# Input combinations and first weights queued singly behind the dense layer, the third block's denominators one dense block earlier, and the last rows inside the first pair

## The chip, the core and the metric

The kernel runs on one core of a Trainium2 chip. The metric is the device time of one execution in microseconds (us). Three runs of the kernel before gave 2571.55, 2571.56 and 2573.55 us; their median is 2571.56 us.

The engines are named as in the profile: PE does matmuls (PEld is its weight load), DVE is the vector engine, ACT the scalar engine, POOL the one called GpSimd, and SP issues most of the DMAs. Each engine takes its instructions in a fixed order, so an instruction that waits keeps back everything behind it on that engine.

## What is computed

Two kinds of layer alternate over 2048 rows of 576 features: linear attention with a softmax feature map, and a dense layer with a squared ReLU. Both are applied twice, with the same weights.

```python
def _A_ref(x, wqkv, w_phi, wo):                    # 32 heads of 18
    q, k, v = split(x @ wqkv)
    pq, pk = q @ w_phi, k @ w_phi                  # per head
    phi_q = concat([softmax(pq), softmax(-pq)])
    phi_k = concat([softmax(pk), softmax(-pk)])
    kv, z = phi_k.T @ v, sum_over_rows(phi_k)      # per head
    den = phi_q @ z + 1e-6
    return ((phi_q @ kv) / den) @ wo

def _B_ref(x, w1, b1, w2, b2):                     # 576 -> 4608 -> 576
    r = relu(x @ w1 + b1)
    return (r * r) @ w2 + b2

x = x + _A_ref(layernorm(x), ...)
x = x + _B_ref(layernorm(x), ...)
x = x + _A_ref(layernorm(x), ...)
x = x + _B_ref(layernorm(x), ...)
```

## The kernel before

**Blocks and order.** The 2048 rows are four blocks of 512 (`TB`), each of four tiles of 128 rows. In layer 0 the dense layer runs over the blocks in the order 3, 2, 0, 1. Layer 1 takes them in the order 1, 0, 3, 2: blocks 1 and 0 go through `g_mlp` one after the other, blocks 3 and 2 together through `g_pair`. In the profile's names `m_1` and `m_0` are the dense blocks of row blocks 1 and 0 (of either layer, as buffer numbers are left out), `a_3` and `a_2` the attention of blocks 3 and 2, and `m_p` the pair. Here "the first dense block" and "the second dense block" mean block 1 and block 0 in layer 1.

**Split numbers.** To keep fp32 accuracy, each matmul operand is split into a rounded high part and the rest, and three products are added. So each operand costs ACT a copy (the high part) and DVE or POOL a subtraction (the rest).

**`g_mlp` (L684).** 36 chunks `f` of 128 hidden features. `first(f)` loads and splits one chunk's weights (DMAs at L695 to L697, ACT L702 and L703, DVE L705 and L706, POOL L707). `hidden(f)` makes 14 products into PSUM bank `h` (L717). `square(f)` empties that bank with a ReLU on ACT (L724), squares it twice on ACT (L725, L726) and takes the rest on DVE (L727); the last of these is kept as `dense["last"]`. `second(f - 1)` adds to five PSUM banks, `acc0` to `acc4` (L735, L744). After each chunk it yields. At the end the features' bank is turned (`m_0py`, L780), added to the rows loaded into `x` tiles (L783, L784), the last chunk's row products for tiles 0 and 1 and then for tiles 2 and 3 follow (L776, L786), and four rows are stored (L789).

**`weave` (L99).** The dense block is the main generator and everything else is traced between its yields. Each yield adds `rate` to a credit, and steps of the other generator are taken while the credit is at least 1; a step costs what it yields (`paced` sets that).

```python
due += rate
while due >= 1.0:
    cost = next(other, other)
    if cost is other:
        break
    due -= cost or 1.0
```

In layer 1 the rates are 3.0 for the first dense block and 4.8 for the second. Costs: 5.5 for one tile's softmax (`g_soft`), 2.8 for each of the eight half-steps of the denominators (`g_phi`: sums over the features, reciprocals, and scaling), 1.0 for a step of queries or of the attention's output (`g_out`), and 3.0 for a step of the norm behind it. A dense block has 36 turns (two after chunk 0, then one a chunk).

**Order.** A scheduler places the traced instructions on each engine by when it holds them ready, the earlier traced ones first. `tc.issue_after(ins)` adds an edge of order alone: what the block traces on `ins`'s engine stands behind `ins` in that engine's queue. `held` (L560) wraps every step of a generator in one such edge, behind `dense["last"]`, so on DVE alone.

**What rides on the second dense block.** For block 3: denominators, output, and `g_norm_first`. For block 2: queries, softmax, denominators, output, and `g_norm_second`. The latter has ten steps: four tiles of rows with their norm, then main steps 0 and 1, a tail, main steps 2 and 3, a tail. A main or tail step turns normed rows on PE into one of the two `w` banks (L814, L822) and makes input combinations of blocks 3 and 2 from them (`combine`: DVE L895 to L900, POOL L901 and L903), each of which is split (L886, L887, L913, L914). Last, `next(pair)` (L1266) runs the first part of `g_pair`: pair 0's weights are loaded (`load_pair`, L937 and L939, ten DMAs) and all seven operands made and split in one go (`split_pair`; POOL sums L970, L972, L975, L977; ACT L962, DVE L963, POOL L965 for each split), and pair 1's weights are loaded.

**`g_pair` (L925).** 18 pairs of chunks. With the combined inputs, seven products (`product`, L997) give a pair's hidden features of both blocks. Three banks are used: `bx` in `h`, `by` and `bz` in the two `w` banks. `bx` is read by DVE between products (L1091, L1100, L1104) that go on adding to it. The next pair's `split_pair` is a generator `prep` with one yield: four splits after the product `s1`, three after `a22`. Its sums are `x` tiles, of which there are five in all; the dense block's end takes four of them.

Of the kernel before, what the change touches and what calls it, by code (L numbers as in the profile page):

```python
# [21 lines left out]
def layers_kernel(  # L22
# [661 lines left out]
    def g_mlp(layer, b, x, after, name, behind=None):  # L684
# [34 lines left out]
        def square(f):  # L719
# [6 lines left out]
            nc.scalar.activation(hr, hr, AF.Square)  # L726
# [54 lines left out]
        for t in range(NT):  # L781
# [3 lines left out]
            after.append(x)  # L785
        by_rows(NF - 1, range(2, NT), range(3))  # L786
# [138 lines left out]
    def g_pair(layer, blocks, x, after, name):  # L925
# [17 lines left out]
        def split_pair(k, raw):  # L943
# [28 lines left out]
            nc.gpsimd.tensor_sub(ss[1], ss[0], a11)  # L972
            split("s2", ss[1])
            yield
            nc.gpsimd.tensor_sub(ss[3], a12, ss[1])  # L975
            split("s4", ss[3])
            nc.gpsimd.tensor_sub(ss[2], a11, a21)  # L977
            split("s3", ss[2])
            split("a22", a22)

# [99 lines left out]
        for k in range(NP):  # L1080
            f0, f1 = 2 * k, 2 * k + 1
            prep = split_pair(k + 1, raw) if k + 1 < NP else iter(())
            bx = ps_a.tile([P, TB], F32, tag="h", name=f"{name}px{k}")
            by = ps_w.tile([P, TB], F32, tag="w", name=f"{name}py{k}")
            bz = ps_w.tile([P, TB], F32, tag="w", name=f"{name}pz{k}")
            load_wide(f0)
            product(k, bx, "a11", "b11", True)
            product(k, by, "a12", "b21", True)
            z = sb.tile([P, TB], F32, tag="hr", name=f"{name}z{f0}", bufs=2)
            nc.scalar.activation(z, by, AF.Copy)  # L1090
            nc.vector.scalar_tensor_tensor(z, bx, bias(f0), z, op0=ALU.add, op1=ALU.add)  # L1091
            nc.scalar.activation(z, z, AF.Relu)
            square(f0, z)
            product(k, bz, "s1", "t1", True)
            next(prep, None)
            product(k, bx, "s2", "t2", False)
            u = sb.tile([P, D], F32, tag="qk", name=f"{name}u{f0}", bufs=5)[:, :TB]
            v = sb.tile([P, D], F32, tag="qk", name=f"{name}u{f1}", bufs=5)[:, :TB]
            nc.scalar.activation(v, bz, AF.Copy)
            nc.vector.tensor_add(u, bx, v)  # L1100
            product(k, by, "s4", "b22", True)
            product(k, bx, "s3", "t3", False)
            nc.vector.scalar_tensor_tensor(u, by, bias(f0), u, op0=ALU.add, op1=ALU.add)
            nc.vector.scalar_tensor_tensor(v, bx, bias(f1), v, op0=ALU.add, op1=ALU.add)  # L1104
            nc.scalar.activation(u, u, AF.Relu)
            nc.scalar.activation(u, u, AF.Square)
            nc.sync.dma_start(hd[f0], u)
            keep_high(f1, v)
            if k:
                second(f0 - 1)  # L1110
            load_wide(f1)
            product(k, bx, "a22", "t4", False)
# [4 lines left out]
            if k + 2 < NP:  # L1117
                raw = load_pair(k + 2)
# [4 lines left out]
        for f in range(NF, NF + 2):  # L1123
            load_wide(f)
            load_high(f)
# [184 lines left out]
```

## Time and profile before

| | value |
|---|---|
| median of 3 runs | 2571.56 us |
| the profiled execution | 2570.49 us |
| its span on the core | 2568.8 us |
| mean granted clock of PE | 0.993 |
| busy in the span: PE, PEld | 2508.2 us (98%), 2205.1 us (86%) |
| DVE, ACT, POOL | 1536.7 us (60%), 1266.5 us (49%), 801.5 us (31%) |
| DMA | 295.03 MB, mean 115 GB/s |

In this trace the first dense block runs from about 1528 to 1798 us, the second from 1798 to 2126 us, the 18 pairs of features from 2126 to 2452 us, and block 2's rows from there to the end.

How to read the lines. In a table of stretches each row has the stretch, its length, the busy time of PE, PEld, DVE, ACT and POOL with their instructions, the granted clock, the DMA share and GB/s. A row of waits has the engine and line that waited, whom for, and total, times and longest in us. A row in order of time has start, duration, engine, line, operation, output and inputs, and in brackets the idle time before it and what ended it. A row of the chain of waits has start, duration and what. PE's ends are modelled and matmuls overlap, so the distance between starts tells more than a duration.

### The profile page before, as it was taken

The numbers are of one execution on the slowest core, as the hardware profiler recorded it, in microseconds if no ns is written. First come the engines' busy times: TensorE is split into PE (matmuls) and PEld (weight loads), VectorE is DVE, ScalarE is ACT, GpSimd is POOL, SyncE is SP. The second block draws the span as 40 slices with busy tenths as digits, with TensorE's granted clock in tenths as the row PEclk, the third lists the DMA queues.
The fourth block names the chain that finished last, engine by engine and source line by source line (L and its number), as shares of the span: only waits on it lengthen the run. The fifth ranks groups of instructions, "written<-read, shape, count | busy, mean of one in ns | idle before, by whom it ended". The sixth has DMA issues, their size and how long they took to land.

```text
span 2568.8 us, 41380 instructions
## 1 busy us (share of the span) xinstructions
PE 2508.2 (98%) x15282; PEld 2205.1 (86%) x15282; DVE 1536.7 (60%) x2408; ACT 1266.5 (49%) x2177; POOL 801.5 (31%) x869
## 2 busy tenths in 40 slices
PE   8998999999999999999999999999999989999999
PEld 8998888888888888888888988888888877888888
DVE  7778844456665467556434787464757765555444
ACT  4344554445554455545544445454545456666543
POOL 3444311113222133223111433112223256555222
PEclk9999999999999999999999999999999999999999
DMA  8103333354333543343333143333453434333364
GB/s 251 57 23 92 102 111 91 109 185 129 92 92 113 171 126 98 88 138 99 111 100 100 45 146 105 89 89 107 141 176 90 124 93 132 115 99 104 103 204 152
DMA packets 276758, 295.03 MB, mean 115 GB/s; under 512 B 28906, under 2 KB 206826, under 8 KB 274250
## 3 DMA queue, kind: packets, MB, share of 16 engines
q1 hardware_dynamic: 275296, 289.68, 37.6%
q8 instruction: 119, 1.95, 0.3%
q10 hardware_dynamic: 1258, 2.70, 0.3%
q14 instruction: 85, 0.70, 0.1%
HBM read 249.39 MB, written 42.89 MB: 114 GB/s over the span
## 4 chain that ended last, share of the span: by engine, by line
PE 52%; DVE 6%; POOL 1%; issue 1%; ACT 1%; DMA 0%; DVEq 0%; ACTq 0%; POOLq 0%; SPq 0%
PE m_1ph L717 9%; PE m_1acc L744 7%; PE m_0ph L717 5%; PE m_ppx L997 5%; PE m_pacc L1026 3%; PE m_0acc L744 3%; PE m_pacacc L1026 3%; PE m_ppy L997 2%; PE m_1acc L735 2%; PE m_ppz L997 1%; PE m_pacacc L1016 1%; PE m_pacc L1016 1%; PE m_0acc L735 1%; PE m_pach L1026 1%; PE a_0po L671 1%
## 5 line engine op out<-in xcount | busy, mean ns | idle before, releaser
L717 PE MATMUL m_0ph<-a_0nh,m_0h 128*128 128x512 f32 (+1 forms) x760 | 198.7, 389 | 8.2 <-ACT m_0hr L724 6.6
L744 PE MATMUL m_0acc<-m_0s,m_0hb 128*128 128x448 f32 x864 | 200.4, 367 | 3.7 <-DVE m_0hb L727 3.7
L744 PE MATMUL m_1acc<-m_1s,m_1hb 128*128 128x448 f32 x864 | 199.2, 366 | 0.5 <-DVE m_1hb L727 0.5
L744 PEld LDWEIGHTS m_0acc<-m_0s,m_0hb 128*128 128x128 f32 x864 | 161.3, 188 | 26.9 <-DVE m_0hb L727 6.0
L744 PEld LDWEIGHTS m_1acc<-m_1s,m_1hb 128*128 128x128 f32 x864 | 162.0, 188 | 21.4 <-DVE m_1hb L727 0.9
L717 PEld LDWEIGHTS m_0ph<-a_0nh,m_0h 128*128 128x128 f32 x760 | 137.5, 191 | 35.3 <-ACT m_0hr L724 7.5
L707 POOL TENSOR_TENSOR m_1s<-m_1r,m_1s 128x128 fp32r<-128x128 f32 x72 | 57.7, 801 | 334.8 <-ACT m_1s L703 298.1
L707 POOL TENSOR_TENSOR m_0s<-m_0r,m_0s 128x128 fp32r<-128x128 f32 x72 | 60.4, 838 | 312.9 <-ACT m_0s L703 280.6
L705 DVE TENSOR_TENSOR m_1h<-m_1r,m_1h 128x640 fp32r<-128x640 f32 x72 | 63.7, 885 | 145.8 <-ACT m_1h L702 145.8
L724 ACT ACTIVATE m_0hr<-m_0ph,b1t 128x512 f32<-128x512 f32 x72 | 49.3, 685 | 166.3 <-PE m_0ph L717 166.3
L705 DVE TENSOR_TENSOR m_0h<-m_0r,m_0h 128x640 fp32r<-128x640 f32 x72 | 65.7, 913 | 100.7 <-ACT m_0h L702 98.6
L724 ACT ACTIVATE m_1hr<-m_1ph,b1t 128x512 f32<-128x512 f32 x72 | 49.4, 685 | 148.5 <-PE m_1ph L717 148.5
L986 DVE TENSOR_TENSOR m_ps<-m_pr,m_ps 128x448 fp32r<-128x448 f32 x72 | 51.2, 711 | 95.8 <-ACT m_ps L985 94.9
L987 POOL TENSOR_TENSOR m_ps<-m_pr,m_ps 128x128 fp32r<-128x128 f32 x72 | 59.0, 819 | 136.2 <-ACT m_ps L985 128.1
L744 PE MATMUL m_2acc<-m_2s,m_2hb 128*128 128x448 f32 x432 | 99.7, 366 | 1.3 <-DVE m_2hb L727 1.3
L744 PE MATMUL m_3acc<-m_3s,m_3hb 128*128 128x448 f32 x432 | 99.6, 366 | 1.0 <-DVE m_3hb L727 1.0
L717 PE MATMUL m_1ph<-t1onh,m_1h 128*128 128x512 f32 (+1 forms) x380 | 97.1, 382 | 0.6 <-ACT t1onh L347 0.6
L717 PE MATMUL m_2ph<-a_2nh,m_2h 128*128 128x512 f32 (+1 forms) x380 | 97.2, 384 | 0.2 <-DVE m_2h L705 0.2
L717 PE MATMUL m_3ph<-t0onh,m_3h 128*128 128x512 f32 (+1 forms) x380 | 95.7, 382 | 0.1
L717 PE MATMUL m_1ph<-a_1nh,m_1h 128*128 128x512 f32 (+1 forms) x380 | 95.2, 381 | 0.0
L1026 PE MATMUL m_pacc<-m_ps,m_phb 128*128 128x448 f32 x432 | 94.1, 366 | 0.0
L985 ACT ACTIVATE m_ps<-m_pr 128x576 fp32r<-128x576 f32 x72 | 49.1, 683 | 88.6 <-PE m_pacacc L1016 63.7
(2103 smaller groups left out, 7121.2 us busy)
## 6 DMA issues: line engine op xcount, KB each, us to landing
m_0r<-in_B_w SPq DMA_DIRECT2D x72, 288.0 KB
m_1r<-in_B_w SPq DMA_DIRECT2D x72, 288.0 KB
m_pr<-in_B_w SPq DMA_DIRECT2D x72, 288.0 KB
m_0r<-in_B_w SPq DMA_DIRECT2D x72, 256.0 KB
m_1r<-in_B_w SPq DMA_DIRECT2D x72, 256.0 KB
m_3r<-in_B_w SPq DMA_DIRECT2D x36, 288.0 KB
m_2r<-in_B_w SPq DMA_DIRECT2D x36, 288.0 KB
m_3r<-in_B_w SPq DMA_DIRECT2D x36, 256.0 KB
```

Source lines behind the costliest of these rows:

```text
L705: nc.vector.tensor_sub(l1, r1, h1.bitcast(F32))
L707: nc.gpsimd.tensor_sub(s2[:, D + R : 2 * D], r2[:, R:], s2[:, R:D].bitcast(F32))
L717: nc.tensor.matmul(ph[:, cols], a, m, start=(k == 0), stop=(k == len(ops) - 1))
L724: nc.scalar.activation(hr, ph, AF.Relu, bias=b1t[:, f : f + 1])
L735: nc.tensor.matmul(acc[KC], a, m, start=(f == 0 and k == 0), stop=(f == NF - 1 and k == 2))
L744: nc.tensor.matmul(acc[t][:, :R], a[:, rows], m, start=(f == 0 and k == 0), stop=(f == NF - 1 and k == 2))
L985: nc.scalar.activation(s2[:, :D], r2, AF.Copy)
L986: nc.vector.tensor_sub(s2[:, D : D + R], r2[:, :R], s2[:, :R].bitcast(F32))
L987: nc.gpsimd.tensor_sub(s2[:, D + R : 2 * D], r2[:, R:], s2[:, R:D].bitcast(F32))
L997: nc.tensor.matmul(ps, a, m, start=start and i == 0, stop=i == len(ms) - 1, skip_group_check=True)
L1016: nc.tensor.matmul(accs[b][KC], a, m, start=(g == 0 and k == 0), stop=(g == NF - 1 and k == 2))
L1026: nc.tensor.matmul(accs[b][t][:, :R], a[:, rows], m, start=(g == 0 and k == 0), stop=(g == NF - 1 and k == 2))
```

## The change

1. `square` also keeps ACT's second square (L726) as `dense["squared"]`, and `held` takes a list of keys: its steps then stand behind the newest chunk's last subtraction on DVE and behind its second square on ACT.
2. `g_norm_second` is run through `held` with both keys.
3. `split_pair` yields after each of its seven splits, and POOL's sums are traced ahead of the split before the one that needs them. Pair 0's splitting is a generator of its own, `prelude`, run through `held` with both keys at a cost of 2.0 a step. In each pair the steps of `prep` are taken two after the first square, two after product `s1`, two before product `a22`, and the rest after it.
4. Block 3's denominators (`g_phi`, eight half-steps of 2.8) move from the second dense block to the first, behind block 3's softmax, which was there already.
5. The rates go from 3.0 to 3.6 for the first dense block and from 4.8 to 4.3 for the second.
6. At the end of the second dense block, ahead of the last chunk's row products for tiles 2 and 3, a new call `then` drains what is left of the side work and traces pair 0 up to its product `a22`. Pair 0 takes its five accumulators only after that.

```diff
-    def held(gen):
+    def held(gen, keys=("last",)):

         while True:
-            with tc.issue_after(dense["last"].ins):
+            with ExitStack() as behind:
+                for key in keys:
+                    behind.enter_context(tc.issue_after(dense[key].ins))
                 cost = next(gen, gen)
...
-            nc.scalar.activation(hr, hr, AF.Square)
+            dense["squared"] = nc.scalar.activation(hr, hr, AF.Square)
             dense["last"] = nc.vector.tensor_sub(hl, hr, hh.bitcast(F32))
...
             after.append(x)
+        if then:
+            then()
         by_rows(NF - 1, range(2, NT), range(3))
...
+            nc.gpsimd.tensor_add(ss[0], a21, a22)
             split("a11", a11)
+            yield
+            nc.gpsimd.tensor_sub(ss[1], ss[0], a11)
             split("a12", a12)
-            nc.gpsimd.tensor_add(ss[0], a21, a22)
+            yield
             split("s1", ss[0])
-            nc.gpsimd.tensor_sub(ss[1], ss[0], a11)
+            nc.gpsimd.tensor_sub(ss[3], a12, ss[1])
+            yield
             split("s2", ss[1])
-            yield
-            nc.gpsimd.tensor_sub(ss[3], a12, ss[1])
+            nc.gpsimd.tensor_sub(ss[2], a11, a21)
+            yield
             split("s4", ss[3])
-            nc.gpsimd.tensor_sub(ss[2], a11, a21)
+            yield
             split("s3", ss[2])
+            yield
             split("a22", a22)
+            yield
...
-        drain(split_pair(0, load_pair(0)))
-        raw = load_pair(1)
-        yield
-        accs[0] = [ps_a.tile([P, TB], F32, tag=f"acc{c}", name=f"{name}acc{c}") for c in range(NC)]
+        def prelude():
+            yield from split_pair(0, load_pair(0))
+            raws[1] = load_pair(1)
...
+                square(f0, z)
+                advance(prep, 2)
+                product(k, bz, "s1", "t1", True)
+                advance(prep, 2)
+                product(k, bx, "s2", "t2", False)
...
+                load_wide(f1)
+                advance(prep, 2)
+                if k == 0:
+                    yield
+                product(k, bx, "a22", "t4", False)
+                drain(prep)
...
+                if k == 0:
+                    accs[0] = [ps_a.tile([P, TB], F32, tag=f"acc{c}", name=f"{name}acc{c}") for c in range(NC)]
+                second(f0)
+                yield
...
+    def g_features(layer, raws, ph, name):
+        cost = (lambda c: c) if layer else (lambda c: None)
+        er = []
+        yield from paced(held(g_soft(raws, er, name)), cost(5.5))
+        yield from paced(held(g_phi(layer, er, ph, name, True)), cost(2.8))
...
-                    mid = (g_queries(layer, order[2], None, later, m), paced(held(g_soft(later, early, m)), 5.5))
+                    mid = (g_queries(layer, order[2], None, later, m), g_features(layer, later, early, m))
...
-                    yield from g_attend(layer, order[3], None, None, operands, f"a{layer}_{order[3]}", None, g_norm_second)
-                    next(pair)
+                    yield from g_attend(layer, order[3], None, None, operands, f"a{layer}_{order[3]}", None,
+                                        lambda *a: held(g_norm_second(*a), ("last", "squared")))
+                    yield from paced(held(prelude, ("last", "squared")), 2.0)
...
-            weave(g_mlp(layer, b, ready, rows, f"m{n}", None if i else dense["turned"]), g_back(), (3.0, 4.8)[i] if layer else 1.5 if i else 1.0)
+            back = g_back()
+
+            def then(back=back):
+                drain(back)
+                next(products)
+
+            weave(g_mlp(layer, b, ready, rows, f"m{n}", None if i else dense["turned"], then if layer and i == 1 else None),
+                  back, (3.6, 4.3)[i] if layer else 1.5 if i else 1.0)
```

More of the change, by code (lines that the diff above doesn't have):

```diff
@@ L681, in g_out, with g_mlp @@
         yield from paced((norm or g_norm)(x_after, dst, f"{name}n", keep), costs[1])
-    def g_mlp(layer, b, x, after, name, behind=None):
+    def g_mlp(layer, b, x, after, name, behind=None, then=None):
         xh, xl = x["h"], x["l"]
@@ L1134, in load_x @@
+        return prelude(), products()
     def load_x(b):
@@ L1148, in g_attend @@
                 yield from g_queries(layer, b, x, raws, name)
-            yield from paced(held(g_soft(raws, er, name)), cost(5.5))
-        ph = []
-        yield from paced(held(g_phi(layer, er, ph, name, True)), cost(2.8))
+            yield from g_features(layer, raws, ph, name)
         if mid[0]:
@@ L1231, in layers_kernel @@
         operands = {}
-        pair = g_pair(layer, order[2:], operands, None, f"m{layer}_p")
+        prelude, products = g_pair(layer, order[2:], operands, None, f"m{layer}_p")
         for i, b in enumerate(order):
```

110 lines of the change are left out of this document (53 added, 57 removed).

## The prediction

> **What bounds the kernel now.** I read the page first, then a table of stretches, then the matrix engine's waits, then the order of time around each wait. The page's first line gives the span; this execution took 2570.49 us in all (1.69 us lie around its span), 1.07 under the median 2571.56 of the three runs.
>
> ```profile
> span 2568.8 us, 41380 instructions
> ```
>
> In the table of stretches (us, then busy time per engine) layer 1's first dense block keeps PE busy throughout, and so do the steady feature pairs; the second dense block, between them, does not.
>
> ```profile
> 1528.00:1798.00 270.00, 270.00 (x1359) 234.69 (x1358) 154.74 (x232) 139.28 (x224) 56.66 (x63) 1.00 0.36 103
> 1798.00:2108.00 310.00, 295.73 (x1553) 254.89 (x1552) 212.47 (x344) 150.55 (x262) 108.77 (x116) 0.99 0.40 124
> 2144.00:2452.00 308.00, 308.00 (x1377) 257.15 (x1376) 152.52 (x252) 191.07 (x351) 152.47 (x199) 1.00 0.36 109
> ```
>
> PE's waits from 1520 to 2160 us (total, times, longest) say what it stood still for:
>
> ```profile
> PE m_0ph L717 <- ACT m_0hr L724: 6.6, 3, 6.0
> PE m_0acc L744 <- DVE m_0hb L727: 2.4, 3, 1.6
> PE a_2np L814 <- DVE a_2nh L887: 2.2, 1, 2.2
> PE m_ppx L997 <- DVE m_pz L1091: 1.9, 1, 1.9
> PE m_ppx L997 <- DVE m_pu L1104: 1.8, 1, 1.8
> PE m_0ph L717 <- DVE m_0h L705: 1.4, 1, 1.4
> PE a_2pn L638 <- DVE a_2fl L625: 0.9, 1, 0.9
> PE a_3pn L638 <- DVE a_3fl L625: 0.6, 1, 0.6
> ```
>
> These eight make 17.8 us, all between 1798 and 2144. Two of them leave the matmuls behind them slow. In the chain of waits one chunk's 14 products take 3.25 us, but 5.89 after the wait of 6.0:
>
> ```profile
> 2101.93 1.00 POOL m_ps L972
> 2103.60 1.08 POOL m_ps L975
> 2104.67 1.14 POOL m_ps L977
> 2106.27 0.72 ACT m_0h L702
> 2107.61 5.89 PE m_0ph L717 x14
> ...
> 2116.62 3.25 PE m_0ph L717 x14
> ```
>
> And after the wait of 2.2 they take 4.68, from their first group to what follows:
>
> ```profile
> 2085.90 2.48 PE L717 MATMUL m_0ph<-a_0nh,m_0h 128*128 128x512 f32 x5
> ...
> 2090.58 1.78 PE L744 MATMUL m_0acc<-m_0s,m_0hb 128*128 128x448 f32 x8
> ```
>
> That is another 2.6 and 1.4 us, so 21.8 us are to be had there at most, in a PE that is otherwise full.
>
> An undisturbed chunk takes 6.34 us (26 of them between these two pieces of the chain):
>
> ```profile
> 1219.81 3.26 PE m_1ph L717 x14
> ...
> 1384.65 3.26 PE m_1ph L717 x14
> ```
>
> The Trainium skill (TensorE: Matmul & The Clock Gate, Part 1) lets the clock fall only after about 3.4 us of idling; here 2.2 us of it sufficed. By the page a remaining wait under 3.4 us would cost only itself, by the rows above one of 2.2 costs 1.4 more.
>
> **The first weights, queued singly.** Today all seven splits of pair 0 are drained in one go. Their POOL sums stand one behind the other (L972, L975 and L977 in the chain above), ACT's copies wait for them in order, and the dense block's own ACT instruction, which empties the bank of the next hidden chunk, stands behind those copies. The change adds none of these 25 instructions and removes none. It makes seven steps of them, costed 2.0 each in a weave of 4.3 per chunk (two steps a chunk), puts each sum a step ahead of its split, and queues ACT and DVE behind the newest chunk's squares. Two steps hold at most two sums of 1.0 to 1.1 us, well under 6.34, so the 6.0 + 2.6 = 8.6 us should shrink to about 0.6. Bounds: 0 and 8.6 saved; I take 8.0, since the block's copy can no longer find four sums ahead of it.
>
> ```profile
> 2094.93 1.86 SPq L939 DMA_DIRECT2D m_pr<-in_B_w  x4
> ```
>
> SP is not held back: a pair's ten loads, eight of them small (2 × 1.86 us of its queue), still go out when their buffers come free, as they do now. Counting the costs written in the code, the block's side work grows from 32.7 of 36 weave turns (156.8 / 4.8) to 34.5 (148.4 / 4.3), so the last split comes at chunk 34 of 35: close, but ahead of the products.
>
> **The input combinations.** They move in the turns too: today main steps 0 and 1 fall in one turn, and 2 and 3 in another; at 4.3 no two mains share one. Now ACT takes a combination's copy, idling 1.85 us for POOL, ahead of the block's square:
>
> ```profile
> 2076.95 0.42 ACT L913 ACTIVATE a_2nt4h<-a_2nu 128x256 fp32r<-128x256 f32 x1 [1.85 <-POOL a_2nu L903]
> ...
> 2077.84 0.62 ACT L725 ACTIVATE m_0hb<-m_0hr 128x512 fp32r<-128x512 f32 x1
> ```
>
> A main step has six POOL instructions like this one:
>
> ```profile
> 2070.56 0.74 POOL L901 TENSOR_TENSOR a_2nu<-a_2nb21h,a_2nu 128x256 f32<-128x256 f32 x1
> ```
>
> The added wait holds the step's DVE and ACT work (evictions, moments, sums, copies) behind `hl` and the second square. That is where a first step already stands (the sub at 2066.74, the combination at 2067.77), and PE has the previous chunk's second half to do meanwhile.
>
> ```profile
> 2065.55 0.83 DVE L705 TENSOR_TENSOR m_0h<-m_0r,m_0h 128x640 fp32r<-128x640 f32 x1 [1.56 <-ACT m_0h L702]
> 2066.74 0.69 DVE L727 TENSOR_TENSOR m_0hb<-m_0hr,m_0hb 128x512 fp32r<-128x512 f32 x1 [0.36 <-ACT m_0hr L726]
> 2067.77 0.43 DVE L895 TENSOR_TENSOR a_2nu<-a_2np,a_2nb11h 128x256 f32<-128x256 f32 x1 [0.34 <-PE a_2np L814]
> 2068.12 0.61 DVE L706 TENSOR_TENSOR m_0s<-m_0r,m_0s 128x448 fp32r<-128x448 f32 x1
> ```
>
> At stake are 2.2 and its 1.4 of slow clock, 0.6 of the wait on L724 (6.6 less 6.0) and about 0.5 of that on L727 (2.4 less 1.6 and some 0.3 earlier): 4.7 us. A main step costs POOL 6 × 0.74 = 4.4 us; two in one turn are more than a turn has, singly they fit. Bounds 0 and 4.7; I take 4.0, nearer the upper one, as only a tail still shares a turn with a main.
>
> **Denominators one layer ahead.** Block 3's eight half-steps leave the start of the second block for the first. Their DVE cost, from two stretches (a chunk's own DVE work is 0.83 + 0.69 + 0.61 = 2.13):
>
> ```profile
> 1568.00:1626.00 58.00, 58.00 (x273) 50.11 (x272) 36.50 (x62) 29.56 (x48) 17.47 (x18) 1.00 0.37 103
> 1801.00:1838.00 37.00, 35.62 (x190) 31.04 (x189) 33.45 (x58) 17.76 (x29) 15.26 (x13) 1.00 0.59 185
> ```
>
> The first, block 0's in the first dense block at 3.0 / 2.8 = 1.07 half-steps a chunk: 36.5 - 9.15 × 2.13 = 17.0, or 2.1 each, with no PE wait. The second, block 3's today at 4.8 / 2.8 = 1.71: 33.45 - 5.84 × 2.13 = 21.0, or 2.6 each. So a chunk now asks DVE for 2.13 + 1.71 × 2.6 = 6.6 us of 6.34: overloaded, and the 1.4 follows. After the change the first block runs at 3.6 / 2.8 = 1.29, that is 4.8 to 5.5 us: hidden behind PE's 6.34. I charge 0.5 for turns that hold two half-steps; with the cover gone it is the second block's own price for both blocks of rows, 2 × (1.4 + 0.6) = 4. The 1.4 goes. The 0.6 is the attention output's start and stays. Block 2's denominators slow to 4.3 / 2.8 = 1.54, 5.4 to 6.1 us; of the 1.6 + 0.3 + 0.9 = 2.8 us there I take 1.5 as saved (bounds 0 and 2.8).
>
> **Last rows in the first pair.** Six row products and the last two stores move behind pair 0's first six products. The waits there are 1.9 and 1.8. ACT's copy of `by` (L1090), on which the first depends, stands behind a split that waits for POOL; POOL's sums wait for an `x` buffer, which comes free when the block's rows are stored:
>
> ```profile
> 2131.53 0.52 ACT L962 ACTIVATE m_pwc_1l<-m_ps 128x384 fp32r<-128x384 f32 x1 [1.36 <-POOL m_ps L975]
> 2131.96 0.58 ACT L1090 ACTIVATE m_pz<-m_ppy 128x512 f32<-128x512 f32 x1
> ```
>
> ```profile
> 2125.93 2.51 DMA out<-m_0x
> 2128.57 1.04 POOL m_ps L972
> ```
>
> That dependence is still there. The second wait gets six moved matmuls in place of six that stand there already. So I take only 1.5 of 3.7 (bounds -1 and 3.7: two of the buffers come free later than now).
>
> **Sum.** 8.0 + 4.0 + 1.4 + 1.5 + 1.5 - 0.5 = 15.9 us; 2570.49 - 15.9 = 2554.6, and 2555.7 beside the median.
>
> **Rivals.** *The wait only shifts.* Issue order is not time: ACT's copies still need POOL's results, and the block's squares can still fall behind one of them. Half of the two large terms and nothing in pair 0: 4.3 + 2.35 + 1.4 + 1.5 - 0.5 = 9.0, so 2562.6. For it speaks the idle 1.85 above, which a later place in the queue does not shorten; against it, that the sums now run a step ahead.
> *Crowded denominators.* A half-step cost DVE 2.1 us spread out and 2.6 crowded. If it is crowded in the first block too and turns with two of them overrun (2.13 + 2 × 2.6 = 7.3 us of 6.34), the price is 4 instead of 0.5: 2559.2. The Trainium skill (GPSIMD Engine Reference, Key points) has a rule to that end: POOL shares its SBUF interfaces with DVE and contends with a DVE instruction that reads two SBUF inputs, as these products do. Against it: the mean of 5.5 is under 6.34, and each chunk's weights are made ready a chunk ahead.
> *It does nothing.* The scheduler takes what is ready, whatever the trace order, so the same stalls appear elsewhere: 2571.6.
> *Slower: the steady pairs.* The same rewrite reorders the splits inside all 18 pairs: sums and splits of the next pair now come before ACT's copies of this one. If pair 0's 1.9 us recurs in the other 17, that is 32.3 against 15.9: 2588. It decides from 15.9 / 17 = 0.94 us a pair. Against it: 308.00 of 308 us PE-busy today with ACT at 191 and POOL and DVE at 152, and splits that wait for their buffers to come free, which the change leaves alone.
>
> **How the numbers follow.** Forecast 0.60, shifted wait 0.17, crowded denominators 0.05, nothing 0.07, steady pairs 0.11. A measurement of this kernel tells 0.2%, about 5 us, from no change; the first three lie beyond it, so faster 0.82, same 0.07, slower 0.11. With every term at its upper bound 21.2 us go, which is 2550.4; with pair 0 at nothing and denominators and combinations at half it is 2560: the forecast's own range. I widen it to 2548 (the waits' small change) and 2566, the top of "faster", to take in the shifted wait; the last two cases, 0.18, stay outside.
>
> **What would show it.** Right: no PE wait on L724 over 1 us ahead of the pairs, no stretch of half clock from 2060 to 2130, first dense block still full of PE work, steady pairs 17.7 us apart, everything from pair 1 on moved up by some 15 us. Wrong: a wait of PE on ACT or DVE in each pair (slower), or over 2 us around the denominators in the first block, or a new wait of the first pair for `x` buffers.

## The result and the profile after

Twenty runs of the changed kernel have a median of 2567.07 us (2564.97 to 2568.99), twenty of the kernel before, on the same chips, 2573.18 (2570.37 to 2575.99). The ratio is 0.9976, with a 95% interval of 0.9969 to 0.9983: 6.1 us faster, just beyond the 0.2% that can be told from no change. The forecast was 15.9 us, with a range of 2548 to 2566 us; the measured median lies 1.1 us above it. The profiled execution took 2566.98 us.

The page's first line of the changed kernel, and its table of stretches (us, then busy time of PE, PEld, DVE, ACT, POOL with their instructions, granted clock, DMA share, GB/s):

```profile
span 2565.3 us, 41355 instructions
```

```profile
1528.00:1798.00 270.00, 269.31 (x1351) 234.39 (x1352) 175.05 (x262) 138.79 (x222) 70.51 (x68) 0.99 0.35 105
1798.00:2108.00 310.00, 301.20 (x1582) 260.53 (x1581) 197.23 (x317) 153.78 (x268) 99.11 (x111) 0.99 0.41 130
2144.00:2452.00 308.00, 308.00 (x1377) 257.16 (x1376) 153.27 (x254) 190.55 (x349) 151.28 (x197) 1.00 0.36 113
```

The first dense block took in the denominators (DVE 154.74 to 175.05 us) and stayed full. The steady pairs are as full as before. The second block gained, from 295.73 to 301.20 us of PE work in 310. Its PE waits, of the changed kernel from 1520 to 2160 us (total, times, longest):

```profile
PE m_ppx L1007 <- DVE m_pu L1122: 3.4, 1, 3.4
PE m_0ph L719 <- ACT m_0hr L726: 3.0, 2, 2.0
...
PE a_2np L818 <- DVE a_2nl L918: 1.7, 1, 1.7
PE a_2pn L640 <- DVE a_2fl L627: 1.2, 1, 1.2
PE m_0acc L746 <- DVE m_0hb L729: 0.9, 2, 0.6
PE a_2pt L624 <- DVE a_2Q3e L594: 0.7, 1, 0.7
```

The wait of 6.0 on the block's own ReLU is gone (L726 now, L724 before), and so are both waits at block 3's denominators and output (L705, and L638 on a_3fl). The transposes' wait (L818 now, L814 before) is there still, 1.7 in place of 2.2; it ends with a main's subtraction (L918) where it ended with a tail's (L887). At the first pair one wait of 3.4 stands where two of 1.9 and 1.8 stood.

Where the stages begin shows how much each gave. In order of time, PE's first product of the second dense block, of pair 0 and of pair 2; before, then after:

```profile
1799.61 0.63 PE L717 MATMUL m_0ph<-a_0nh,m_0h 128*128 128x256 f32 x4
...
2126.53 0.63 PE L997 MATMUL m_ppx<-a_2nb11h,m_pwv 128*128 128x512 f32 x2
...
2163.02 0.61 PE L997 MATMUL m_ppx<-a_2nb11h,m_pwv 128*128 128x512 f32 x2
```

```profile
1802.22 0.63 PE L719 MATMUL m_0ph<-a_0nh,m_0h 128*128 128x256 f32 x4
...
2119.30 0.71 PE L1007 MATMUL m_ppx<-a_2nb11h,m_pwv 128*128 128x512 f32 x2
...
2158.66 0.62 PE L1007 MATMUL m_ppx<-a_2nb11h,m_pwv 128*128 128x512 f32 x2
```

The second block fell from 326.92 to 317.08 us (1.22 of it, six row matmuls, moved into pair 0), and the first two pairs grew from 36.49 to 39.36: 7.0 us gained in all. The remaining pairs take what they took. These distances can be compared between kernels; the times at which they begin cannot: in the sixteen profiled executions of this study the first dense block began anywhere from 1519.8 to 1524.6 us, behind work that no edit is aimed at. It took either 278.8 to 279.2 or 279.9 to 280.3 us, whether block 3's denominators were in it (278.80 to 280.27) or not (278.93 to 280.18). The nine long ones, and none of the seven short ones, have 3.4 us of half clock near their start. The changed kernel's:

```profile
1530.20:1533.60 3.40, 3.40 (x18) 3.38 (x17) 0.36 (x1) 0.45 (x1) 0.00 (x0) 0.50 0.79 246
```

### The profile page after: what moved, and what is told of

Its sections match the earlier page's. It is cut to its first block, busy times and chain, and to the rows that moved or that the text cites. A ratio compares the mean times of both kernels' runs of the same rounds, so it can differ in the third digit from the quotient of the medians.

```text
span 2565.3 us, 41355 instructions
## 1 busy us (share of the span) xinstructions
PE 2508.4 (98%) x15282; PEld 2205.9 (86%) x15282; DVE 1540.2 (60%) x2408; ACT 1268.4 (49%) x2177; POOL 804.9 (31%) x869
## 3 DMA queue, kind: packets, MB, share of 16 engines
q1 hardware_dynamic: 275296, 289.68, 36.7%
## 5 line engine op out<-in xcount | busy, mean ns | idle before, releaser
L709 POOL TENSOR_TENSOR m_0s<-m_0r,m_0s 128x128 fp32r<-128x128 f32 x72 | 59.5, 826 | 316.0 <-ACT m_0s L705 279.9
L726 ACT ACTIVATE m_0hr<-m_0ph,b1t 128x512 f32<-128x512 f32 x72 | 49.3, 685 | 169.8 <-PE m_0ph L719 169.8
L726 ACT ACTIVATE m_1hr<-m_1ph,b1t 128x512 f32<-128x512 f32 x72 | 49.5, 688 | 152.7 <-PE m_1ph L719 152.7
```

The source lines that it names most:

```text
L709: nc.gpsimd.tensor_sub(s2[:, D + R : 2 * D], r2[:, R:], s2[:, R:D].bitcast(F32))
L726: nc.scalar.activation(hr, ph, AF.Relu, bias=b1t[:, f : f + 1])
```

## The experiments

All of them in one table: the second dense block, the first two pairs and their sum from each kernel's trace (distances as above), the difference of the medians within its own comparison, and the ratio to the kernel before with its interval. In the kernels marked * the six row matmuls (1.22 us) lie in pair 0 and not in the block. One trace stands for each kernel, so a difference under 1 us of the sums, or 2 us of the times, is not read as anything.

| kernel | block | two pairs | sum | time | ratio |
|---|---|---|---|---|---|
| before | 326.92 | 36.49 | 363.41 | | |
| after * | 317.08 | 39.36 | 356.44 | -6.1 | 0.9976 (0.9969 to 0.9983) |
| e1_hold_alone | 327.28 | 38.01 | 365.29 | -0.9 | 1.0001 (0.9992 to 1.0010) |
| e2_free_combos * | 316.95 | 39.37 | 356.32 | -8.9 | 0.9969 (0.9957 to 0.9980) |
| e3_rows_last | 317.85 | 37.65 | 355.50 | -7.3 | 0.9968 (0.9955 to 0.9980) |
| e4_bank_first * | 313.64 | 40.73 | 354.37 | -10.7 | 0.9961 (0.9948 to 0.9973) |
| e5_sum_first * | 316.60 | 39.60 | 356.20 | -5.8 | 0.9976 (0.9967 to 0.9985) |
| e7_phi_back * | 321.79 | 39.56 | 361.35 | -2.2 | 0.9993 (0.9984 to 1.0002) |
| e9_t4_pool * | 317.38 | 40.50 | 357.88 | -6.2 | 0.9972 (0.9962 to 0.9982) |
| e12_prelude_once * | 318.13 | 37.67 | 355.80 | -6.9 | 0.9969 (0.9959 to 0.9979) |
| e14_room_alone | 319.15 | 36.39 | 355.54 | -8.6 | 0.9965 (0.9952 to 0.9977) |
| e15_steps_alone | 320.82 | 40.30 | 361.12 | -4.5 | 0.9983 (0.9974 to 0.9992) |
| e16_bank_rows | 315.44 | 36.77 | 352.21 | -11.6 | 0.9952 (0.9939 to 0.9964) |
| e17_room_bank | 317.40 | 38.16 | 355.56 | -10.0 | 0.9960 (0.9947 to 0.9974) |
| e18_room_fast | 321.90 | 38.17 | 360.07 | -4.9 | 0.9981 (0.9973 to 0.9990) |
| e19_bank_rows_free | 315.46 | 36.69 | 352.15 | -12.5 | 0.9950 (0.9936 to 0.9963) |

### The input combinations: the hold, or what stands in ACT's queue

The forecast held that the added edges take 4.0 us off the combinations. In the changed kernel's order of time one turn with a main and a tail reads:

```profile
2070.17 0.42 ACT L917 ACTIVATE a_2nt4h<-a_2nu 128x256 fp32r<-128x256 f32 x1 [1.81 <-POOL a_2nu L907]
2070.50 0.37 ACT L917 ACTIVATE a_2nh<-a_2np 128x256 fp32r<-128x256 f32 x1
2070.67 0.73 POOL L918 TENSOR_TENSOR a_2nt4l<-a_2nu,a_2nt4h 128x256 fp32r<-128x256 f32 x1 [0.53 <-ACT a_2nt4h L917]
...
2070.89 0.43 DVE L918 TENSOR_TENSOR a_2nl<-a_2np,a_2nh 128x256 fp32r<-128x256 f32 x1 [1.99 <-ACT a_2nh L917]
...
2071.47 0.63 PE L818 MATMUL a_2np<-ident,a_2nn 128*128 128x128 f32 x4 [1.68 <-DVE a_2nl L918]
...
2073.16 1.22 PE L719 MATMUL m_0ph<-a_0nh,m_0h 128*128 128x512 f32 x2 [1.07 <-ACT m_0hr L726]
```

ACT idles 1.81 us for POOL's chain ahead of t4's copy. Behind it in the queue stands the copy of b22 (`a_2nh<-a_2np`), which needs nothing of POOL, reads the PSUM bank, and lets DVE free it; PE's next transposes wait for that bank. The block's L726 stands there too.

e1 puts only the hold into the kernel before.

```diff
 (kernel before)
+            with ExitStack() as behind:
+                for key in keys:
+                    behind.enter_context(tc.issue_after(dense[key].ins))
...
-                    yield from g_attend(layer, order[3], None, None, operands, f"a{layer}_{order[3]}", None, g_norm_second)
+                    yield from g_attend(layer, order[3], None, None, operands, f"a{layer}_{order[3]}", None,
+                                        lambda *a: held(g_norm_second(*a), ("last", "squared")))
```

> The kernel before with one edit: the input combinations of block 3 are held behind the dense layer's subtraction and second square; the prelude, the denominators, the rates and the last rows stay as before. If the forecast's price of the hold was right (4.0 us gained), the second dense block falls from 326.9 to about 322.9 us and the time by about 4. If the hold only puts the wait in another place (the transposes then wait for the PSUM bank, because the copies that free it start behind the dense layer's work and stand behind a copy that waits for POOL), the block stays at 326.9 +- 1.2 and the time within 1.5 us of before, with a PE wait of over 1 us on L906 (or the line of the transposes) that the kernel before does not have.

The block stayed (327.28). The wait on the ReLU grew from 6.0 to 7.1, and the transposes' from 2.2 to 2.5. PE's waits of that kernel from 1800 to 2126 us:

```profile
PE m_0ph L719 <- ACT m_0hr L726: 7.5, 2, 7.1
PE a_2np L816 <- DVE a_2nh L889: 2.5, 1, 2.5
```

e2 takes the hold out of the changed kernel (`g_norm_second` in place of the `lambda`).

> The changed kernel with the input combinations not held, all else as changed; PE's order is the same. In the changed kernel PE loses 6.7 us in the two turns that hold a main and a tail (4.6 around 2062 to 2077 us, 2.1 at 2088). If the hold helps as forecast, that loss grows by about 4 (second dense block 321, time +4). If the hold is what makes the bank late, the loss falls by 2 to 5 us (block 312 to 315, time -2 to -5). If it is the packing, a main and a tail in one turn, whatever their order on DVE, the loss stays within 1 us of 6.7 (block 317 +- 1).

317.0 against 317.1 for the block, 356.3 against 356.4 for the sum: the hold is worth nothing either way. (The times lie 2.8 us apart, -8.9 and -6.1, but their intervals overlap, and the distances show no such gain.)

e4 changes one place in ACT's queue.

```diff
 (changed kernel)
+            seen = None
             for k, src in combine((p4[:, 0], p4[:, 1]), *old):
                 hi, lo = (p[:, :, rows] for p in ops[k][:2])
-                nc.scalar.activation(hi, src, AF.Copy)
+                with tc.issue_after(seen.ins) if k == "t4" else nullcontext():
+                    copied = nc.scalar.activation(hi, src, AF.Copy)
+                seen = copied if k == "b22" else seen
```

> The changed kernel, and in each main of the combinations ScalarE's copy of t4 (which waits for POOL's chain of four) is put behind the copy of b22 (which reads the PSUM bank and waits for nothing on POOL). If the bank is late because b22's copy stands behind t4's, the transposes' wait of 1.7 us at the bank and the half clock behind it go: PE's loss of 4.6 us at 2062 to 2077 falls to 1 to 2, the second dense block from 317.1 to about 314, the time by 2 to 3.5. The wait of 2.1 at 2088 stays, or goes too if L726 no longer stands behind a waiting t4 (then 4 to 5 in all). If it is the packing of the turn, the block stays at 317.1 +- 1.

The block fell by 3.4, as the bank's theory had it; the pairs gave 1.4 of it back. Its order of time shows the two copies swapped, the transposes without a wait, and what is left: L726 behind the copy that waits.

```profile
2065.13 0.38 ACT L919 ACTIVATE a_2nh<-a_2np 128x256 fp32r<-128x256 f32 x1
...
2066.44 0.60 PE L818 MATMUL a_2np<-ident,a_2nn 128*128 128x128 f32 x4
2066.98 0.42 ACT L919 ACTIVATE a_2nt4h<-a_2nu 128x256 fp32r<-128x256 f32 x1 [1.16 <-POOL a_2nu L907]
...
2068.89 0.96 PE L719 MATMUL m_0ph<-a_0nh,m_0h 128*128 128x512 f32 x3 [1.85 <-ACT m_0hr L726]
```

e9 tries to take that one too: t4's high part is copied on POOL.

```diff
 (changed kernel; the same in split_tail for the tails)
-                nc.scalar.activation(hi, src, AF.Copy)
+                if k == "t4":
+                    nc.gpsimd.tensor_copy(hi, src)
+                else:
+                    nc.scalar.activation(hi, src, AF.Copy)
```

> The changed kernel, and the first copy of t4 (the high part, in the mains and in the tails) is made on POOL, right behind POOL's own sum, in place of ScalarE, which then waits for POOL nowhere in the combinations. With ScalarE's order alone mended (t4's copy behind b22's) the second dense block took 313.6 us in place of 317.1, and a wait of 1.8 us was left, where the dense layer's relu L726 stood behind t4's copy. If ScalarE's waiting for POOL is the whole of the combinations' loss, that wait goes too: loss 6.7 to about 1, block 311 to 312, time 5 to 6 below the changed kernel. If the bank was all that counted, it does as well as the mended order (block 313.6). If POOL becomes the bound (a copy of about 0.7 us more in each of its chains of 4.4), the transposes or the pairs wait for POOL and the block stays above 315.

This missed its aim: the block took 317.4, as the expectation's last case had it. The turn at 2070 lost nothing now, but a wait of 1.9 at 2079 is new, and a tail's split on DVE waits for POOL in ACT's place, 3.35 us, and the block's own subtraction, behind it, comes late for PE:

```profile
2091.35 1.22 DVE L894 TENSOR_TENSOR a_2nt4t<-a_2nu,a_2nt4t 32x256 fp32r<-32x256 f32 x1 [3.35 <-POOL a_2nt4t L891]
...
2095.21 0.94 DVE L729 TENSOR_TENSOR m_0hb<-m_0hr,m_0hb 128x512 fp32r<-128x512 f32 x1
...
2096.20 1.36 PE L746 MATMUL m_0acc<-m_0s,m_0hb 128*128 128x448 f32 x4 [2.96 <-DVE m_0hb L729]
```

### The first weights: the single steps, or the room

The wait of 6.0 is gone in the changed kernel. What took it away? e12 undoes the single steps and their hold alone; e7 takes the denominators back into the second block, with the rates of before.

```diff
 (e12: changed kernel)
-                    yield from paced(held(prelude, ("last", "squared")), 2.0)
+                    drain(prelude)
 (e7: changed kernel)
-                    mid = (g_queries(...), g_features(layer, later, early, m))
+                    mid = (g_queries(...), paced(held(g_soft(later, ers, m)), 5.5))
...
+        elif not ph:
+            yield from paced(held(g_phi(layer, ers, ph, name, True)), cost(2.8))
...
-                  back, (3.6, 4.3)[i] if layer else 1.5 if i else 1.0)
+                  back, (3.0, 4.8)[i] if layer else 1.5 if i else 1.0)
```

> The changed kernel with the first pair's weights made ready in one go again, not held and not in steps, at the end of the weave. If the forecast's price of the single steps was right (8.0 us) and stands by itself, PE loses about 8.7 us in place of 0.8 at the end of the second block, which grows from 317.1 to about 325, and the time grows by 8. If the room in the turns does as much as the steps (in the run with block 3's denominators back in this block the steps still cost 3.6), it grows by 4 to 6 alone.

> The changed kernel with block 3's denominators in the second dense block again, and the rates of before (3.0 and 4.8); held combinations, the prelude in single steps and the last rows in the first pair stay. If the move was worth what the traces' difference says, the first dense block falls by 1.0 (279.9 to 278.9), the second grows by 2.3, from 317.1 to about 319.4, and the time by about 1.3. If the 1.0 in the first dense block is not the denominators' (they ran beside a full PE there), the first block stays at 279.9 and the time grows by 2.3. If the packing of main and tail in one turn is the combinations' loss, it changes with the rates, since main and tail then fall in other turns: in the kernel before it was 5.6 in place of 6.7.

Both expectations fell. Without the steps the block grew by 1.05 and the pairs shrank by 1.7: nothing lost. With the denominators back it cost 4.9 in all, not 1.3 or 2.3, and the first block was no shorter. So the move carried more than its own waits. e14 and e15 put each part alone into the kernel before.

```diff
 (e14: kernel before; g_features as in the change)
-                    mid = (g_queries(...), paced(held(g_soft(later, early, m)), 5.5))
+                    mid = (g_queries(...), g_features(layer, later, early, m))
...
-                                        g_norm_first, er=early)
+                                        g_norm_first, ph=early)
...
-(3.0, 4.8)[i] if layer else 1.5 if i else 1.0)
+(3.6, 4.3)[i] if layer else 1.5 if i else 1.0)
 (e15: e7 without the hold of the combinations and without `then`)
```

> The kernel before with the move of block 3's denominators into the first dense block and the rates 3.6 and 4.3, and nothing else: the first weights in one go and unheld, the combinations unheld, the last rows ahead of the first pair. By the forecast this part is worth 2.4 us (1.4 and 1.5 less 0.5): second dense block 326.9 to about 324, time about 2571. If it is the room that counts (with the denominators gone, the first weights come two turns of the weave earlier, and no two mains share a turn), the block falls to 317 to 319 and the time by 6 to 8, to about 2566: the whole effect of the change.

> The kernel before with the new split_pair in single held steps at the end of the weave (and the new places of the later pairs' splits that come with it), and nothing else: denominators, rates, combinations and last rows as before. By the forecast this part is worth 8.0 us: second dense block 326.9 to 319, time about 2565. If it is the room that counts, the steps only spread the wait: with the held combinations besides, PE still lost 3.6 us there in place of 8.7, so the block falls to 321 to 323, and two us of that go again in the first pair: time 2569 to 2571.

The move with its rates gives 7.9 us by the trace, all that the change gives. The steps alone take 6.1 off the block, and the first pairs give 3.8 of it back. The orders of time show why both can remove the same wait. Before, POOL works through two mains with hardly a break (twelve instructions of 0.73 to 0.92 us, first and last here), and the first weights' sums come behind them:

```profile
2089.52 0.74 POOL L914 TENSOR_TENSOR a_2nt1l<-a_2nu,a_2nt1h 128x256 fp32r<-128x256 f32 x1 [1.93 <-ACT a_2nt1h L913]
...
2097.90 0.75 POOL L914 TENSOR_TENSOR a_2nt3l<-a_2nu,a_2nt3h 128x256 fp32r<-128x256 f32 x1
...
2105.84 0.52 ACT L962 ACTIVATE m_pwa<-m_ps 128x384 fp32r<-128x384 f32 x1 [0.61 <-POOL m_ps L977]
2106.89 0.67 ACT L724 ACTIVATE m_0hr<-m_0ph,b1t 128x512 f32<-128x512 f32 x1
```

In e14 the same instructions, in one go and unheld, end 11 us earlier (14 counted from the block's start), and the ReLU, behind all four copies as before, finds them done in time:

```profile
2093.16 1.20 POOL L977 TENSOR_TENSOR m_ps<-m_pr 128x384 f32<-128x384 f32 x1
...
2094.39 0.53 ACT L962 ACTIVATE m_pwa<-m_ps 128x384 fp32r<-128x384 f32 x1 [0.63 <-POOL m_ps L977]
2095.45 0.67 ACT L724 ACTIVATE m_0hr<-m_0ph,b1t 128x512 f32<-128x512 f32 x1
```

e18 asks whether coming earlier is enough, or whether the two mains must part: rate 4.8 in place of 4.3 in e14. By the code's costs main 2 and main 3 then share a turn again, and the first weights come three turns earlier still.

> The kernel before with the move of block 3's denominators and the rates 3.6 and 4.8 (4.3 where the move stood alone). Main 2 and main 3 of block 2's combinations share a turn again, as in the kernel before; the first weights come three turns earlier than at 4.3. If the room is what counts, the end of the second block loses no more than at 4.3 (2 us in place of 8.7), and the block stays at 318 to 320. If it is the packing, the two mains in one turn cost what they cost before, and the first weights find POOL busy again: block 323 to 326, time 2569 or more.

Neither rival had it: 321.9, between the two. On POOL the two mains stand ahead of the sums as in the kernel before (twelve instructions again, and 16.5 us from the first of them to the end of the last sum, 16.3 before). But the block's ReLU now stands behind only the first of the four copies, and PE waits 1.9 us for it and 1.5 for the next, where it waited 6.0:

```profile
2060.18 0.74 POOL L914 TENSOR_TENSOR a_2nt1l<-a_2nu,a_2nt1h 128x256 fp32r<-128x256 f32 x1 [1.40 <-ACT a_2nt1h L913]
...
2068.59 1.13 POOL L914 TENSOR_TENSOR a_2nt3l<-a_2nu,a_2nt3h 128x256 fp32r<-128x256 f32 x1
...
2072.79 0.67 ACT L724 ACTIVATE m_0hr<-m_0ph,b1t 128x512 f32<-128x512 f32 x1
...
2076.74 0.52 ACT L962 ACTIVATE m_pwa<-m_ps 128x384 fp32r<-128x384 f32 x1 [0.26 <-POOL m_ps L977]
```

So the wait of 6.0 took two things together: late sums, and a ReLU behind all four copies that wait for them. In e14 the first is gone, in e18 the second.

Coming earlier with the mains together gives 5.0 us of the block's 7.8, the moved denominators' own waits of 1.4 and 0.6 among it; the slower rate gives the other 2.8, a good part of it at block 2's denominators, where a wait of 1.6 on L727 is back. By the sums, to which the pairs add, it is 3.3 and 4.5. PE's waits in e18:

```profile
PE m_0ph L717 <- ACT m_0hr L724: 3.3, 2, 1.9
PE a_2np L814 <- DVE a_2nh L887: 2.1, 1, 2.1
...
PE m_0acc L744 <- DVE m_0hb L727: 2.0, 2, 1.6
```

### The first pair

The chain to the wait of 3.4 in the changed kernel, in order of time:

```profile
2131.57 1.19 POOL L979 TENSOR_TENSOR m_ps<-m_pr,m_ps 128x384 f32<-128x384 f32 x1
2132.79 0.52 ACT L966 ACTIVATE m_pwa<-m_ps 128x384 fp32r<-128x384 f32 x1 [1.34 <-POOL m_ps L979]
...
2133.35 0.63 DVE L967 TENSOR_TENSOR m_pwa<-m_ps,m_pwa 128x256 fp32r<-128x256 f32 x1 [1.44 <-ACT m_pwa L966]
...
2133.91 0.74 DVE L1122 SCALAR_TENSOR_TENSOR m_pu<-m_ppx,b1t,m_pu 128x512 f32<-128x512 f32 x1
```

Pair 0's last sum stands behind a split of pair 2, which waits for ACT, which waits for POOL. e3 puts the rows back ahead of pair 0 (no `then`). e5 holds pair 2's splits behind that sum.

```diff
 (e5: changed kernel)
                 prep = split_pair(k + 1, raws.pop(k + 1)) if k + 1 < NP else iter(())
+                if k == 1:
+                    prep = held(prep, ("summed",))
...
-                nc.vector.scalar_tensor_tensor(v, bx, bias(f1), v, op0=ALU.add, op1=ALU.add)
+                summed = nc.vector.scalar_tensor_tensor(v, bx, bias(f1), v, op0=ALU.add, op1=ALU.add)
+                if k == 0:
+                    dense["summed"] = summed
```

> The changed kernel with the dense layer's last rows ahead of the first pair again, as before, and not inside it (six row matmuls, 1.22 us, go back into the second block: 317.1 to 318.3). If the rows inside the pair bring the new wait of 3.4 us at L1122, the first pair falls from 21.6 to 18.7 us or less (as before) and the time by about 1.7. If pair 2's weights, made ready too early, bring it, the wait stays, now with 1.2 us less work to cover it, besides the z wait of about 2 us that the kernel before had: the first pair takes 21.5 to 23.5, and the time grows by 1 to 3.

> The changed kernel, and pair 2's weights (the splits made during pair 1's turn of the program) are held behind the first pair's last sum, L1122. In the changed kernel that sum stands on DVE behind a split of pair 2 that waits for ScalarE's copy, which waits for POOL's sums, and PE waits 3.4 us for it and runs 1.3 us longer at the lower clock behind the gap. If that order is the cause, the wait falls below 0.8 us, the first pair from 21.6 to 17.5 to 18.5, the time by 3 to 4. If the buffers of the rows (POOL's sums wait for a store to give one back) or the moved rows are the cause, the wait stays above 2 us.

e5 did to pair 0 what was expected and nothing to the time. Its stretches, pair 0 and pair 1:

```profile
2117.80:2134.50 16.70, 16.45 (x73) 12.96 (x71) 10.31 (x19) 9.98 (x20) 11.18 (x15) 1.00 0.42 132
2134.50:2157.40 22.90, 19.72 (x79) 15.84 (x79) 14.24 (x21) 11.93 (x23) 16.23 (x19) 0.93 0.41 126
```

Pair 0 fell to 16.7 us and pair 1 grew from 17.7 to 22.9. POOL's load went along: 11.18 us in pair 0 and 16.23 in pair 1, where the changed kernel has 16.74 and 11.33. It looks as if two pairs' sums have to be made while the pairs start, and whichever pair they fall in pays; no run made POOL's own work less. e3 took 37.65 us for both pairs, not the 21.5 to 23.5 for the first that the backlog's theory gave (it took 19.9), nor the 18.7 of the other, and 0.9 less in all than the changed kernel: the moved rows gain nothing.

### Together

e16 is e4 with the rows ahead of pair 0, e19 is e16 without the hold, e17 is e14 with e4's edit.

> The changed kernel with two edits at once, tried singly already: ScalarE's copy of t4 behind that of b22, and the last rows ahead of the first pair. If they add, the second dense block takes 313.6 + 0.8 = 314.4, the first two pairs 37.7 us, and from the second block's start to the end of pair 1 it is 352 us in place of 356.4: time about 2562, the best of these. If the backlog is what counts and only shifts, it is 354 to 356 and no better than the copy's order alone (354.4).

> The kernel before with the move and the rates (as in the run that has them alone), and ScalarE's copy of t4 behind that of b22: two small edits, without the single steps, the holds and the moved rows. If the room and the bank's order are what there is to gain, it does as well as the changed kernel with the copy's order mended, or better: second block 313 to 316, first two pairs 36.5 to 38, time 2561 to 2564. If the single steps are needed besides, PE loses 4 us or more at the end of the second block and the time stays above 2566.

> The changed kernel with the copy of t4 behind that of b22, the last rows ahead of the first pair, and the combinations not held. With the hold these two edits gave 2562.65 us and 315.4 us for the second block, with 2.0 us lost at the combinations in one wait and no half clock. If the hold is worth the 4.0 of the forecast once the bank is freed in time, the block grows to 319; if it is worth nothing, it stays at 315.4 +- 1; if the hold itself makes the transposes late, the block falls to 313 or 314.

The two edits of e16 add up: 352.2, as forecast, and the time is 11.6 us below the kernel before. In e17 the copy's order takes 1.8 off the block, which at 317.4 misses the 313 to 316 expected, and the pairs give it back. e19 is as good as e16 in the trace (315.5 and 36.7) and has the lowest time, 2561.52 us, 12.5 below the kernel before; the 0.9 us between them is not read as anything. With the bank freed in time the hold is still worth 0.0.

## Why the prediction was wrong

**First weights, 8.0.** The wait went, as forecast, with its slow clock. The step that failed: "Two steps hold at most two sums of 1.0 to 1.1 us, well under 6.34, so the 6.0 + 2.6 = 8.6 us should shrink to about 0.6". It priced the steps as if they stood alone and were the only way. Added alone they take 6.1 us off the block but bring 2.3 in all (e15), and taken out of the change they cost nothing (e12). The prediction looked at which instructions stand ahead of the ReLU on ACT, not at why their sums were late: twelve POOL instructions of two mains stood ahead of them. The wait needed both, and the move and its rates, priced for something else, took it away without the steps (e14).

**Input combinations, 4.0.** The hold came to nothing: 0.1 (e2), 0.0 (e19), and 1.9 lost by the trace where it stood alone (e1; the ratio of its times, 1.0001, shows no loss). The step that failed: "The added wait holds the step's DVE and ACT work ... behind `hl` and the second square", taken as a gain. The work that hurt did not start too early; ACT waited for POOL in the middle of it. The row that the prediction quoted, t4's copy idling 1.85 us for POOL, was the cause of 3.4 us in the block (e4), and it was 1.81 after the change. The rival "the wait only shifts" named just that.

**Denominators, 1.4 less 0.5, and 1.5 for the slower rate.** The first block stayed full, as forecast, and the 0.5 is not to be seen. The waits of 1.4 and 0.6 both went. But the part was sized at 2.4 and measured 7.9 (e14). The prediction counted that the side work would fill 34.5 of 36 turns, and that no two mains share a turn, and gave the credit for it to the two holds. Block 2's denominators and output still lose what they lost (1.6 + 0.3 + 0.9 before; 1.2 + 0.7 + 0.4 and a part of 0.9 after); at the faster rate it would be more (e18), so the slower rate pays for coming earlier there.

**Last rows in the first pair, 1.5.** The pairs lost 1.65 (39.36 - 1.22 - 36.49), a little beyond the bound of -1 that was given. The step that failed: "That dependence is still there", ACT's copy of `by` behind a split that waits for POOL. In the changed kernel that wait went (1.9 before); the new one of 3.4 came by another path, pair 2's splits ahead of pair 0's sum on DVE (e5). And what lost was not the moved rows but, by the runs, the single, held steps of the first weights: with the rows in pair 0 and no such steps the pairs lose nothing (e12, 37.67 - 1.22 = 36.45), with the steps and the rows ahead of it they lose 1.2 (e3) or 3.8 (e15).

The steady pairs, the first dense block and the absence of a wait in each pair came out as written. Of the marks listed beforehand, "no PE wait on L724 over 1 us" failed: 2.0 at a turn with a main and a tail. So did two more: there was half clock at 2073, and pair 1 moved up by 4.3 us (2145.26 to 2140.93), not by 15. "Crowded denominators" and "slower: the steady pairs" are refuted by the stretches above; "it does nothing" by the interval. "The wait only shifts" was right for the combinations. For the first weights it was wrong in the change as a whole, and right in great part for the steps alone, which gave 3.8 of 6.1 us back in the pairs.

What stays open: why the start of the pairs takes 36.4 us in e14 and 38.2 in e17 and e18, which have the same instructions there. The five `x` buffers, POOL's sums and the stores of the block's rows meet in it, and no run took them apart.

## What to carry to other kernels

When PE waits behind a chain of engines, ask two things: how long the last one in the chain (here POOL) had been busy without a break, and how much of what waits for it stands ahead of the instruction that PE needs. Edits that shorten the backlog and edits that spread the waiting instructions remove the same wait, and their prices must not be added. In an in-order queue look for an instruction that waits for another engine while independent work, such as a copy that frees a bank, stands behind it: swapping the two was worth 2.1 us by the sums (e4), holding all of them nothing. And a gain at the end of one stage counts only after the start of the next has been looked at: the first pairs gave back 1.7 to 3.8 us.

## What the runs showed of the hardware

The lower clock comes in whole stretches. In all sixteen traces PE's granted clock is 1.00 or 0.50, and from the first dense block to the last 10 us every stretch at 0.50 lasts 3.4 us or twice that. Whether one follows a gap does not go by the gap's length alone. After a wait of 1.85 us in e4 one began 0.9 us after PE's work did; after 2.65 us in e5, at 2089, none came. At pair 0 the same wait of 3.4 to 3.5 us brought one in the changed kernel and in e2 (from 2133.6), and two in a row (6.8 us) in e4. Stretches of e4, e5, the changed kernel and e4 again:

```profile
2069.80:2073.20 3.40, 3.40 (x10) 2.63 (x9) 2.72 (x6) 1.85 (x4) 0.90 (x1) 0.50 0.23 62
```

```profile
2089.00:2099.00 10.00, 9.30 (x41) 7.58 (x42) 9.94 (x12) 7.94 (x17) 9.49 (x11) 1.00 0.36 107
```

```profile
2134.40:2137.80 3.40, 3.10 (x7) 2.48 (x8) 2.48 (x5) 2.24 (x5) 2.69 (x4) 0.50 0.31 90
```

```profile
2127.80:2134.60 6.80, 5.77 (x15) 4.85 (x16) 4.01 (x7) 4.88 (x9) 5.93 (x8) 0.50 0.54 184
```

The Trainium skill (TensorE: Matmul & The Clock Gate, Part 1) has the activity watched in a free-running window of about 3.4 us, so that the point at which the clock changes depends on where in it the work falls. The lengths and the scatter here agree with that. The same part of the Trainium skill has the half clock come after at least one idle window of that length; a gap of 1.85 us that was enough does not fit that.

POOL's sums can stretch DVE. The split L967, 128x256 with both operands in SBUF, of the changed kernel from 2117 to 2160 us, where POOL's sums crowd, and those of `m_pwa` from 2200 to 2400 in the steady pairs (duration min, median and max in ns):

```profile
L967 DVE TENSOR_TENSOR m_pwv<-m_pr,m_pwv x2: 426/832/1237, 2121.8 to 2125.6; 128x256 fp32r<-128x256 f32 x2
L967 DVE TENSOR_TENSOR m_pwc_1l<-m_ps,m_pwc_1l x2: 679/920/1160, 2126.8 to 2128.0; 128x256 fp32r<-128x256 f32 x2
...
L967 DVE TENSOR_TENSOR m_pwa<-m_ps,m_pwa x10: 425/425/426, 2225.3 to 2369.7; 128x256 fp32r<-128x256 f32 x10
```

The same form of instruction takes up to 2.9 times as long. In that trace the five splits of this form with no POOL work beside them took 411 to 415 ns, and the two over 1 us ran beside one of POOL's 128x384 sums; others beside POOL were not stretched (424 ns). The Trainium skill (GPSIMD Engine Reference, Key points) says that the two engines share their SBUF interfaces and contend when DVE reads two SBUF inputs; the trace agrees. A subtraction with one operand in PSUM, 0.43 us at 2070.89 above beside POOL's work from 2070.67, was not stretched.
